# Gated mix of local attention and a mixture of experts on one core: inputs turned by DVE transposes in place of TensorE's, and the first expert prepared earlier

## The chip, the cores and the metric

The kernel runs on one core of one Trainium2 chip. The metric is the device time of one execution in microseconds (us), the median of the runs shown. PE is TensorE (PEld its weight loads), DVE is VectorE, ACT ScalarE, POOL GpSimd, SP SyncE; SP issues most DMAs and SPq is its DMA queue.

## The reference, cut to what matters

x has 2048 tokens of 512 features. `a` is a dilated local attention (32 heads of 16, a window of 8 at a step of 2), `b` a mixture of the best two of 8 experts with hidden size 1376; a gate mixes them.

```python
g = _sigmoid((x * gate_w).sum(-1, keepdims=True))
qkv = x @ wqkv                      # 512 x 1536, then attention per head
a = attention(qkv) @ wo             # 512 x 512
logits = xf @ w_gate                # 512 x 8
topk_idx = jnp.argsort(-logits, axis=-1)[:, :K]    # K = 2, gates by softmax
for e in range(E):
    h = _silu(xf @ w1[e]) @ w2[e]   # 512 x 1376, 1376 x 512
    out = out + w * h
return g * a + (1 - g) * b
```

## The kernel before, in words

Every float32 product is made of three: each operand is split into a high part (an ACT copy to the float32r type) and a low part (a DVE subtraction), and PE sums high by high, high by low and low by high. PE contracts over partitions, so x must be turned: features on partitions.

**Projection.** Four passes c = 0 to 3 over the 16 row blocks j of x (`qkv_mm` L230, 12 products a block, columns of 8 heads a pass; pass 0 also has the router's and the gate's 10 columns). In pass 0 each block is loaded (`load_x` L114, two blocks a DMA, two buffers), turned by four PE transposes into PSUM and split (`trans_x` L216, two blocks ahead of its products). `load_w` (L124) brings the weights of a pass in four DMAs into one buffer, `split_w` (L201) splits them during the pass before. SP's queue runs in program order (L131 to L135, L192 to L199, L810 to L825): first x and the weights, then the table and halo stores, which wait for POOL's memsets, then more x, the weights of pass 1, the stores of the staged results (L255) and the clearing of the accumulator (L199). POOL loads the gate weights (L141, L142) after one iota and before its other constants. Pass 0's first product needs them, split by `split_wg` (L209). ACT copies each block's result to a staging tile (`qkv_evac` L240); for c > 0 and j < 8 two of the three lie in the memory of the x buffers.

**Routing** runs on DVE in pass 1 (`route_a`, `slots`, `table`, `route_c`); `TQ` holds, for each slot of an expert, row numbers of quarter rows of x, `TG` whole rows.

**Attention** is a list of DVE steps (`att_steps` L513, eight rounds, mostly 2.29 us a step), dealt out between other work by `att_fill` (L579): it keeps a model clock for PE and for DVE, adds the PE time and the DVE time that the caller names, and emits steps until DVE's clock has reached PE's:

```python
clk["dve"] = max(clk["dve"], clk["pe"] - IDLE) + dve
clk["pe"] += pe
while not attn["done"] and clk["dve"] < clk["pe"]:
```

**Experts.** Eight experts in the order ORD = [3, 0, 1, 2, 4, 5, 6, 7], 11 units each (88 units, 0 to 87; a unit is 128 hidden columns). In unit i PE does the first product of unit i + 1 (`g1_mm`, 12 products for 512 tokens), then the second of unit i (`g2_mm`); ACT applies silu twice and DVE makes the low half of the hidden tile (`g1_act` L756). `prep_w1`, `prep_w2` copy weights on ACT and queue the subtractions in `LO`, which `los` (L696) emits. `gather_x` (L647) fetches an expert's tokens on POOL's queue and `prep_x` (L669) turns and splits them, during units 3 to 7 of the expert before. Both have two ways: for the first four experts of the order (`DVT` L46) four gathers of quarter rows and a 32x32 block transpose on DVE; for the last four one gather of whole rows and four PE transposes. The first expert is prepared in pass 3: its first weights are loaded at (c, j) = (3, 0) (L857 to L860), its blocks turned from j = 11 (L869), and unit 2's first weights after the pass (L909).

**End.** In unit 87 the steps of attention that are left are emitted (L941), ACT and DVE split the first two blocks of the attention output (`split_o` L900), then ACT scales the last expert's outputs (`y_out` L780) and POOL adds them into `acc_d`. `acc_d` is loaded back (L969), PE multiplies by wo (`wo_mm` L976, 16 blocks), DVE mixes and SP stores (`mix` L988).

Of the kernel before, what the change touches and what calls it, by code (L numbers as in the profile page):

```python
# [7 lines left out]
F32 = mybir.dt.float32  # L8
# [18 lines left out]
E = 8  # L27
# [11 lines left out]
CRPAD, PAPAD = 160, 64  # L39
# [5 lines left out]

DVT = ORD[:4]  # L46
T_T = 0.43
# [11 lines left out]
def kernel(  # L59
# [41 lines left out]

    phT = ExitStack()
# [10 lines left out]

    def load_x(j0, n):  # L114
        t = pa2.tile([P, 2, D], F32, tag="xr", bufs=2, name=f"xr{j0}")
        nc.sync.dma_start(t[:, :n], xt[:, j0:j0 + n])
        for i in range(n):
            XR[j0 + i] = (t, i)

    NW = [394, 384, 384, 384]  # L120
    wq = wqkv.rearrange("(k p) (t c) -> p k t c", p=P, t=3)
    WR, WH, WL = {}, {}, {}

    def load_w(c, ks=range(KD)):  # L124
        if 0 in ks:
            WR[c] = pa.tile([P, KD, 384], F32, tag="wr", bufs=1, name=f"wr{c}")
        for k in ks:
            nc.sync.dma_start(WR[c][:, k].rearrange("p (t c) -> p t c", t=3),
                              wq[:, k, :, c * P:(c + 1) * P])
# [7 lines left out]

    ii = at.tile([P, P], I32, name="ii", tag="acc")
    nc.gpsimd.iota(ii, pattern=[[1, P]], base=0, channel_multiplier=-1)
    wgr = cp.tile([P, KD, 10], F32, name="wgr")  # L140
    nc.gpsimd.dma_start(wgr[:, :, 0:8], w_gate.rearrange("(k p) e -> p k e", p=P))  # L141
    nc.gpsimd.dma_start(wgr[:, :, 8:9], gate_w.rearrange("(k p o) -> p k o", p=P, o=1))  # L142
    nc.gpsimd.memset(wgr[:, :, 9:10], 0.0)
# [12 lines left out]
    ident = cp.tile([P, P], F32, name="ident")  # L156
    nc.vector.tensor_scalar(ident, ii, 0.0, None, op0=OP.is_equal)
    before = cp.tile([P, P], BF, name="before")
    nc.vector.tensor_scalar(before, ii, 0.0, None, op0=OP.is_gt)
# [40 lines left out]

    def split_w(c, k):  # L201
# [14 lines left out]
    def trans_x(j):  # L216
        t, i = XR[j]
        p = ph(f"px{j}")
        for k in range(KD):
            nc.tensor.transpose(p[:, k * P:(k + 1) * P], t[:, i, k * P:(k + 1) * P], ident)  # L220
        pool = pa2 if j < 8 else pa
        XH[j] = pool.tile([P, KD * P], F32R, name=f"xh{j}")
        XL[j] = pool.tile([P, KD * P], F32R, name=f"xl{j}")
        nc.scalar.activation(XH[j], p, AF.Copy)
        nc.vector.tensor_tensor(XL[j], p, XH[j].bitcast(F32), op=OP.subtract)
# [200 lines left out]
    def table():  # L426
# [6 lines left out]
        V.tensor_scalar(TG, tk[:, 1], float(-NJ), float(S - 1), op0=OP.add, op1=OP.min)  # L433
# [172 lines left out]
    def load_w1(R, i):  # L606
# [4 lines left out]
        if R not in DVT:  # L611
            nc.sync.dma_start(t[:, :, :cols],
                              w1[bass.ds(e, 1), :, f0 * P:f0 * P + cols].rearrange("e (k p) f -> p (e k) f", p=P))
        for a in range(4 if R in DVT else 0):
            nc.sync.dma_start(t[32 * a:32 * a + 32, :, :cols],
                              w1[bass.ds(e, 1), a * P:(a + 1) * P, f0 * P:f0 * P + cols].rearrange("e (k q) f -> q (e k) f", q=32))
# [15 lines left out]
    TG = cp.tile([P, E * NB], I32, name="TG")  # L632
# [14 lines left out]
    def gather_x(R, b):  # L647
        t = cr.tile([P, 4, P], F32, tag="xg", bufs=4, name=f"xg{R}_{b}")
        col = NB * R + b
        XG[R, b] = t  # L650
        if R not in DVT:
            n = blocks(R)[b]
            nc.gpsimd.indirect_dma_start(
                out=t.rearrange("p t c -> p (t c)")[:n], out_offset=None, in_=xf,
                in_offset=bass.IndirectOffsetOnAxis(ap=TG[:n, col:col + 1], axis=0))
            return
        for T in range(-(-blocks(R)[b] // 32)):
            nc.gpsimd.indirect_dma_start(  # L658
                out=t[:, T], out_offset=None, in_=xq,
                in_offset=bass.IndirectOffsetOnAxis(ap=TQ[:, T, col:col + 1], axis=0))  # L660

# [7 lines left out]
    def prep_x(R, b):  # L669
# [4 lines left out]
        if R not in DVT:  # L674
            n = blocks(R)[b]
            t = XG[R, b].rearrange("p t c -> p (t c)")
            p = ph(f"pg{R}_{b}")
            for k in range(KD):
                nc.tensor.transpose(p[:, k * P:k * P + n], t[:n, k * P:(k + 1) * P], ident[:n, :n])  # L679
            pv = p.rearrange("p (k t) -> p k t", k=KD)[:, :, :n]  # L680
            s = slice(b * P, b * P + n)
            nc.scalar.activation(XGH[R][:, :, s], pv, AF.Copy)
            V.tensor_tensor(XGL[R][:, :, s], pv, XGH[R][:, :, s].bitcast(F32), op=OP.subtract)
            return
# [9 lines left out]
    LO = []  # L694
# [116 lines left out]
    for j in range(NJ):  # L811
# [97 lines left out]
    prep_w1(*units[2])  # L909
    los()  # L910
    next_w1(*units[2])
    g1_mm(*units[0])
    g1_act(*units[0], 0)
    for i, (R, f) in enumerate(units):
# [32 lines left out]
        first = T_MM * 12 if C <= 512 else 12 * (C / 2400 + 2 * T_HALF)  # L947
        att_fill(FILL * (first + second))
# [8 lines left out]
        if new_x:  # L957
            prep_x(NEXT[R], f - 3)
# [3 lines left out]
        att_fill((1 - FILL) * (first + second) + (T_T if new_x and NEXT[R] not in DVT else 0.0), T_S + 0.1 + (T_S * (1 + (NEXT[R] in DVT)) if new_x else 0.0))  # L962
# [123 lines left out]
```

## Time and profile before

| | us |
|---|---|
| median of 3 runs (729.88 to 734.13) | 731.86 |
| the profiled execution, its own time | 731.6 |
| its span | 729.8 |
| PE, DVE, ACT, POOL busy | 711.4, 598.7, 339.6, 204.8 |
| TensorE's granted clock, mean over the span (1 is full speed) | 0.992 |

The span is what the profile covers; 1.8 us of the execution's time lie around it. Busy times overlap. A row in order of time gives start, duration, engine, line, operation and tiles, and in brackets how long the engine had been idle and what released it. Matmuls are pipelined: successive ones start closer together than one lasts.

### The profile page before, as it was taken

To read this page: it belongs to the slowest core of one execution; us is meant where nothing else is said; L and a number is where in the kernel's file an instruction comes from. 1 tells how busy PE (TensorE), PEld (TensorE's weight loads), DVE (VectorE), ACT (ScalarE), POOL (GpSimd) and SP (SyncE) were. 2 spreads that over 40 slices of the span, in tenths; PEclk is the share of its full clock that TensorE was granted. 3 is DMA by queue.
4 is the path that set the end of the run, shared out by engine and by line. 5 is a ranking of instruction groups with operands and counts; after the bars stand their busy time and mean duration, and the time that the engine had idled before them with its cause. 6 is when DMAs were issued, how large, how long until landed. Compare 5 with 4: busy or idle time off the path is not lost.

```text
span 729.8 us, 10775 instructions
## 1 busy us (share of the span) xinstructions
PE 711.4 (97%) x3748; PEld 627.1 (86%) x3748; DVE 598.7 (82%) x728; ACT 339.6 (47%) x775; POOL 204.8 (28%) x217
## 2 busy tenths in 40 slices
PE   8999999959999999999999999999999999999996
PEld 7999999958889998999899988888888888888875
DVE  3247799778799988998899999979997999795474
ACT  4443233244645445534553554455446344734531
POOL 3000055062445460731082018206412300300400
PEclk9999999979999999999999999999999999999999
DMA  6668845939386637754675347664665633721592
GB/s 192 183 208 269 219 123 146 251 104 227 101 199 116 154 88 176 136 137 98 166 143 155 122 119 171 185 165 91 166 175 168 132 111 105 154 60 64 79 352 89
DMA packets 81448, 111.34 MB, mean 153 GB/s; under 512 B 7200, under 2 KB 54672, under 8 KB 81008
## 3 DMA queue, kind: packets, MB, share of 16 engines
q1 hardware_dynamic: 73008, 93.21, 45.2%
q0 software_dynamic: 8384, 17.43, 13.1%
q8 instruction: 30, 0.49, 0.3%
q14 instruction: 26, 0.21, 0.1%
HBM read 80.82 MB, written 29.78 MB: 152 GB/s over the span
## 4 chain that ended last, share of the span: by engine, by line
PE 82%; DVE 7%; DMA 6%; issue 2%; ACT 2%; SPq 0%; POOL 0%; DVEq 0%; ACTq 0%; POOLq 0%
PE phh L742 32%; PE py L772 10%; PE py L773 10%; PE py L775 10%; PE pq L237 4%; PE pq L236 4%; PE pq L238 4%; DVE lg L527 2%; DVE pr L524 1%; DMA w2r<-in_B_w_dram 1%; PE pa L984 1%; PE pa L985 1%; PE pa L986 1%; DMA w1r<-in_B_w_dram 1%; PE pg L679 1%
## 5 line engine op out<-in xcount | busy, mean ns | idle before, releaser
L794 POOL DMA_INDIRECT acc_d<-ysb,TI x35 | 94.2, 2691 | 251.5 <-ACT ysb L787 244.2
L772 PE MATMUL py<-w2h,hs 128*128 128x512 f32 (+1 forms) x352 | 138.9, 395 | 0.0
L773 PE MATMUL py<-w2l,hs 128*128 128x512 f32 (+1 forms) x352 | 137.5, 391 | 0.0
L753 ACT ACTIVATE hs<-phh 128x512 fp32r<-128x512 f32 (+7 forms) x121 | 55.8, 489 | 138.7 <-PE phh L742 136.4
L742 PE MATMUL phh<-xgh,w1h 128*128 128x512 f32 (+7 forms) x484 | 99.6, 338 | 8.3 <-ACT xgh L689 7.5
L658 POOL DMA_INDIRECT xg<-in_A_x_dram,TQ x69 | 81.3, 1179 | 89.7 <-DVE xraw L688 69.2
L742 PE MATMUL phh<-xgl,w1h 128*128 128x512 f32 (+7 forms) x484 | 99.3, 338 | 0.0
L742 PE MATMUL phh<-xgh,w1l 128*128 128x512 f32 (+7 forms) x484 | 99.2, 338 | 0.0
L742 PEld LDWEIGHTS phh<-xgh,w1h 128*128 128x128 f32 (+1 forms) x484 | 78.8, 187 | 20.9 <-ACT xgh L689 7.8
L775 PE MATMUL py<-w2h,hs 128*128 128x512 f32 (+1 forms) x352 | 94.2, 389 | 0.0
L756 DVE TENSOR_TENSOR hs<-hsf,hs 128x512 fp32r<-128x512 f32 (+1 forms) x88 | 60.3, 685 | 35.4 <-ACT hsf L755 35.1
L236 PE MATMUL pq<-wh,xh 128*128 128x384 f32 (+1 forms) x256 | 87.7, 343 | 0.0
L722 ACT ACTIVATE w2h<-w2r 128x512 fp32r<-128x512 f32 (+1 forms) x88 | 55.5, 631 | 68.4 <-PE py L775 43.7
L237 PE MATMUL pq<-wl,xh 128*128 128x384 f32 (+1 forms) x256 | 86.2, 337 | 0.2 <-DVE wl L207 0.2
L238 PE MATMUL pq<-wh,xl 128*128 128x384 f32 (+1 forms) x256 | 86.1, 336 | 0.0
L742 PEld LDWEIGHTS phh<-xgl,w1h 128*128 128x128 f32 (+1 forms) x484 | 77.5, 187 | 9.4
L742 PEld LDWEIGHTS phh<-xgh,w1l 128*128 128x128 f32 (+1 forms) x484 | 77.5, 187 | 9.4
L775 PEld LDWEIGHTS py<-w2h,hs 128*128 128x128 f32 (+1 forms) x352 | 66.1, 188 | 13.9
L772 PEld LDWEIGHTS py<-w2h,hs 128*128 128x128 f32 (+1 forms) x352 | 66.1, 188 | 12.7
L773 PEld LDWEIGHTS py<-w2l,hs 128*128 128x128 f32 (+1 forms) x352 | 66.2, 188 | 12.6
L524 DVE TENSOR_TENSOR pr<-qt,kt 128x2048 f32<-128x2048 f32 x32 | 72.7, 2288 | 5.0 <-DMA kt<-qkv 4.6
L527 DVE TENSOR_REDUCE lg<-pr 128x128 f32<-128x2048 f32 x32 | 72.7, 2278 | 0.0
(189 smaller groups left out, 1085.6 us busy)
## 6 DMA issues: line engine op xcount, KB each, us to landing
w2r<-in_B_w_dram SPq DMA_DIRECT2D x40, 512.0 KB, 5.2
qkv<-stg SPq DMA_DIRECT2D x24, 512.0 KB, 4.8
w1r<-in_B_w_dram SPq DMA_DIRECT2D x48, 192.0 KB, 4.5
w1r<-in_B_w_dram SPq DMA_DIRECT2D x12, 768.0 KB, 5.0
kt<-qkv SPq DMA_DIRECT2D x32, 156.0 KB, 6.1
vt<-qkv SPq DMA_DIRECT2D x32, 156.0 KB, 5.7
acc_d<-zer SPq DMA_DIRECT2D x16, 256.0 KB, 4.3
qt<-qkv SPq DMA_DIRECT2D x32, 128.0 KB, 6.0
```

The lines of the kernel that those rows point to most:

```text
L236: nc.tensor.matmul(p[:, :n], XH[j][:, s], WH[c][:, k, :n], start=(k == 0), stop=False)
L237: nc.tensor.matmul(p[:, :n], XH[j][:, s], WL[c][:, k, :n], start=False, stop=False)
L238: nc.tensor.matmul(p[:, :n], XL[j][:, s], WH[c][:, k, :n], start=False, stop=(k == KD - 1))
L524: V.tensor_tensor(pr, qb, custom(k, 4 * u * DH, [[2 * DH, 2], [1, 1024]]), op=OP.mult)
L527: V.tensor_reduce(lg[:, :, 2 * u - 2:2 * u].rearrange("p a w -> p w a"), prs[u - 1].rearrange("p w (a d) -> p w a d", d=16), axis=AX.X, op ...
L658: nc.gpsimd.indirect_dma_start(out=t[:, T], out_offset=None, in_=xq, in_offset=bass.IndirectOffsetOnAxis(ap=TQ[:, T, col:col + 1], axis=0))
L742: nc.tensor.matmul(t[:m, :n], w[:, k, :m], xx[:, k, o:o + n], start=(k == 0 and i == 0), stop=(k == KD - 1 and i == 2))
L756: V.tensor_tensor(hs[:m, 640:1152], s[:m, :512], hs[:m, :512].bitcast(F32), op=OP.subtract)
L772: nc.tensor.matmul(y[b], hs[:m, b * P:(b + 1) * P], wh[:m], start=st, stop=False)
L773: nc.tensor.matmul(y[b], hs[:m, b * P:(b + 1) * P], wl[:m], start=False, stop=False)
L775: nc.tensor.matmul(y[b], hs[:m, 640 + b * P:640 + (b + 1) * P], wh[:m], start=False, stop=sp)
L794: d = nc.gpsimd.indirect_dma_start(out=acc_d, out_offset=bass.IndirectOffsetOnAxis(ap=TI[:n, NB * R + b, 0:1], axis=0), in_=s[:n], in_offs ...
```

## The change

x, the projection's weights and the gate weights are loaded in four DMAs of 32 partitions where one had 128, so that each row block lies in SBUF as 32x32 squares; a DVE transpose in place of four PE transposes turns it (`trans_x`), and ACT and DVE split it from SBUF. Half of pass 0's weights are issued by ACT. The gate weights are issued by POOL ahead of its iota, in eight DMAs. `ident` and `before` are made at j = 4. All experts are gathered by quarters and turned by DVE; `DVT`, `TG` and `T_T` are gone. In an expert's unit `prep_x` now stands at the unit's start, its subtraction goes through `LO`, and DVE's clock is charged in `prep_x` and `los` (T_S = 0.69 each). The first expert's weights are loaded at (2, 6), (2, 8), (2, 10), (2, 12), its blocks prepared from (3, 8), its first weights split from (3, 10), with the loads that follow one block later.

```diff
-CRPAD, PAPAD = 160, 64
+CRPAD, PAPAD = 136, 64
...
-DVT = ORD[:4]
-T_T = 0.43
...
+    xj = xf.rearrange("(t i j) (a c) -> a j i t c", t=4, i=32, a=4)
...
     def load_x(j0, n):
-        t = pa2.tile([P, 2, D], F32, tag="xr", bufs=2, name=f"xr{j0}")
-        nc.sync.dma_start(t[:, :n], xt[:, j0:j0 + n])
+        t = pa2.tile([P, 2, 4, P], F32, tag="xr", bufs=2, name=f"xr{j0}")
         for i in range(n):
-            XR[j0 + i] = (t, i)
+            for a in range(4):
+                nc.sync.dma_start(t[32 * a:32 * a + 32, i], xj[a, j0 + i])
+            XR[j0 + i] = t[:, i]
...
         for k in ks:
-            nc.sync.dma_start(WR[c][:, k].rearrange("p (t c) -> p t c", t=3),
-                              wq[:, k, :, c * P:(c + 1) * P])
+            for a in range(4):
+                (nc.scalar if (c, ks[0]) == (0, 0) else nc.sync).dma_start(
+                    WR[c][32 * a:32 * a + 32, k].rearrange("p (t c) -> p t c", t=3), wq[a, k, :, :, c * P:(c + 1) * P])
...
+    wgr = cp.tile([P, KD, 10], F32, name="wgr")
+    for a in range(4):
+        nc.gpsimd.dma_start(wgr[32 * a:32 * a + 32, :, 0:8], w_gate.rearrange("(a k q) e -> a q k e", a=4, k=KD)[a])
+    for a in range(4):
+        nc.gpsimd.dma_start(wgr[32 * a:32 * a + 32, :, 8:9], gate_w.rearrange("(a k q o) -> a q k o", a=4, k=KD, o=1)[a])
+    nc.gpsimd.memset(wgr[:, :, 9:10], 0.0)
     ii = at.tile([P, P], I32, name="ii", tag="acc")
     nc.gpsimd.iota(ii, pattern=[[1, P]], base=0, channel_multiplier=-1)
-    wgr = cp.tile([P, KD, 10], F32, name="wgr")
-    nc.gpsimd.dma_start(wgr[:, :, 0:8], w_gate.rearrange("(k p) e -> p k e", p=P))
-    nc.gpsimd.dma_start(wgr[:, :, 8:9], gate_w.rearrange("(k p o) -> p k o", p=P, o=1))
-    nc.gpsimd.memset(wgr[:, :, 9:10], 0.0)
...
     def trans_x(j):
-        t, i = XR[j]
-        p = ph(f"px{j}")
-        for k in range(KD):
-            nc.tensor.transpose(p[:, k * P:(k + 1) * P], t[:, i, k * P:(k + 1) * P], ident)
...
-        nc.scalar.activation(XH[j], p, AF.Copy)
-        nc.vector.tensor_tensor(XL[j], p, XH[j].bitcast(F32), op=OP.subtract)
+        b = XR[j].rearrange("p t (k q) -> p t k q", k=KD)
+        nc.vector.transpose(b, b)
+        b = b.rearrange("p t k i -> p k t i")
+        h, l = (t.rearrange("p (k t i) -> p k t i", k=KD, t=4) for t in (XH[j], XL[j]))
+        nc.scalar.activation(h, b, AF.Copy)
+        nc.vector.tensor_tensor(l, b, h.bitcast(F32), op=OP.subtract)
...
     def prep_x(R, b):
...
-        if R not in DVT:
-            n = blocks(R)[b]
-            t = XG[R, b].rearrange("p t c -> p (t c)")
-            p = ph(f"pg{R}_{b}")
-            for k in range(KD):
-                nc.tensor.transpose(p[:, k * P:k * P + n], t[:n, k * P:(k + 1) * P], ident[:n, :n])
...
-            return
         n = -(-blocks(R)[b] // 32)
...
+        clk["dve"] += T_S
         nc.scalar.activation(XGH[R][:, :, s], raw, AF.Copy)
-        V.tensor_tensor(XGL[R][:, :, s], raw, XGH[R][:, :, s].bitcast(F32), op=OP.subtract)
+        LO.append((XGL[R][:, :, s], raw, XGH[R][:, :, s]))
...
-            if (c, j) == (3, 0):
-                for i in range(2):
-                    load_w1(ORD[0], i)
-                    load_w2(ORD[0], i)
+            if c == 2 and j in (6, 8, 10, 12):
+                (load_w1 if j % 4 == 2 else load_w2)(ORD[0], (j - 6) // 4)
             if (c, j) >= ATT0:
-                own = T_S if c < 3 and j in SPLIT[c] else 0.0
-                if c == 3 and j > 10:
-                    own += T_S * 2
-                att_fill(T_P, own)
+                att_fill(T_P, T_S if c < 3 and j in SPLIT[c] else 0.0)
...
-            if c == 3 and j > 10:
-                if j - 11 < len(blocks(ORD[0])):
-                    prep_x(ORD[0], j - 11)
-                if j >= 12:
-                    u = units[(j - 12) // 2]
-                    prep_w1(*u) if j % 2 == 0 else prep_w2(*u)
-                    los()
-                    next_w1(*u) if j % 2 == 0 else next_w2(*u)
+            if c == 3:
+                los()
+                for g, u in NEXTW.pop(j - 1, ()):
+                    g(*u)
+                if 8 <= j < 8 + len(blocks(ORD[0])):
+                    prep_x(ORD[0], j - 8)
+                if 10 <= j < 15:
+                    u = units[(j - 10) // 2]
+                    a, b = (prep_w1, next_w1) if j % 2 == 0 else (prep_w2, next_w2)
+                    a(*u)
+                    NEXTW[j] = ((b, u),)
+    los()
     phA.close()
...
-    prep_w1(*units[2])
-    los()
-    next_w1(*units[2])
     g1_mm(*units[0])
...
+        if new_x:
+            prep_x(NEXT[R], f - 3)
         att_fill(FILL * (first + second))
         los()
...
-        if new_x:
-            prep_x(NEXT[R], f - 3)
         g2_mm(R, f, i)
...
-        att_fill((1 - FILL) * (first + second) + (T_T if new_x and NEXT[R] not in DVT else 0.0), T_S + 0.1 + (T_S * (1 + (NEXT[R] in DVT)) if new_x else 0.0))
+        att_fill((1 - FILL) * (first + second), T_S + 0.1)
```

## Rows read from the trace of the kernel before

**Rows 1.** The page, part 1: busy us, share of the span, instructions.

```profile
PE 711.4 (97%) x3748; PEld 627.1 (86%) x3748; DVE 598.7 (82%) x728; ACT 339.6 (47%) x775; POOL 204.8 (28%) x217
```

**Rows 2.** Windows: busy PE, PEld, DVE, ACT, POOL, then granted clock, DMA share, GB/s.

```profile
154.00:156.00 2.00, 0.00 (x0) 0.00 (x0) 1.67 (x3) 1.31 (x5) 1.54 (x2) 0.62 0.16 47
```

**Rows 3.** PE in order of time at the first expert's start.

```profile
159.57 2.08 PE L742 MATMUL phh<-xgh,w1h 128*128 128x512 f32 x4 [7.49 <-ACT xgh L689]
...
164.79 0.40 PE L742 MATMUL phh<-xgh,w1h 128*128 128x512 f32 x1
```

**Rows 4.** DVE in order of time before it.

```profile
138.40 1.23 DVE L559 TENSOR_TENSOR o<-acc 128x1024 f32<-128x1024 f32 x1
144.26 2.29 DVE L524 TENSOR_TENSOR pr<-qt,kt 128x2048 f32<-128x2048 f32 x1 [4.64 <-DMA kt<-qkv]
```

**Rows 5.** The chain that ended last, at unit starts: start, us, what.

```profile
446.77 2.72 PE phh L742 x12
...
452.21 2.72 PE phh L742 x12
...
458.12 2.72 PE phh L742 x12
```

**Rows 6.** PE in order of time in pass c = 0, and pass 1's first product.

```profile
7.28 0.43 PE L236 MATMUL pq<-wh,xh 128*128 128x394 f32 x1
...
41.42 0.60 PE L220 MATMUL px<-ident,xr 128*128 128x128 f32 x4
...
44.03 0.60 PE L220 MATMUL px<-ident,xr 128*128 128x128 f32 x4
...
48.81 0.33 PE L236 MATMUL pq<-wh,xh 128*128 128x384 f32 x1
```

**Rows 7.** Groups by line: busy us, mean ns; the last line: KB, us to landing.

```profile
L688 DVE STREAM_TRANSPOSE xraw<-xg 128x512 f32<-128x512 f32 x16 | 11.2, 702 | 0.0
L690 DVE TENSOR_TENSOR xgl<-xraw,xgh 128x512 fp32r<-128x512 f32 x16 | 11.1, 692 | 11.2 <-ACT xgh L689 11.2
L689 ACT ACTIVATE xgh<-xraw 128x512 fp32r<-128x512 f32 x16 | 10.1, 632 | 45.0 <-DVE xraw L688 45.0
L141 POOL DMA_DIRECT2D wgr<-in_B_w_gate_dram x1 | 1.0, 977 | 0.4 <-issue 0.4
L854 POOL DMA_DIRECT2D ovx<-ovx_i x1 | 0.6, 571 | 89.1 <-DVE rt_ad L478 89.1
wgr<-in_B_w_gate_dram POOLq DMA_DIRECT2D x1, 16.0 KB, 3.7
```

**Rows 8.** SP's issues: ns min/median/max by line; landing of expert weight quarters; stores in time.

```profile
L116 SPq DMA_DIRECT2D xr<-in_A_x_dram x9: 328/362/1152, 0.8 to 34.4; - x9
L510 SPq DMA_DIRECT2D kt<-qkv x32: 302/419/1058, 73.5 to 561.8; - x32
L128 SPq DMA_DIRECT2D wr<-in_A_wqkv_dram x16: 545/665/1450, 1.2 to 89.0; - x16
w1r<-in_B_w_dram SPq DMA_DIRECT2D x16, 112.0 KB, 2.8
7.33 1.56 SPq L196 DMA_DIRECT2D qkv<-zer  x4
29.82 3.42 SPq L255 DMA_DIRECT2D qkv<-stg  x3
```

**Rows 9.** DVE in order of time at the end.

```profile
657.17 2.31 DVE L565 STREAM_TRANSPOSE ot<-o 128x2048 f32<-128x2048 f32 x1
...
674.30 0.69 DVE L756 TENSOR_TENSOR hs<-hsf,hs 96x512 fp32r<-96x512 f32 x1 [3.59 <-ACT hsf L755]
```

**Rows 10.** ACT in order of time at the end.

```profile
675.20 2.17 ACT L905 ACTIVATE oh<-ot 128x512 fp32r<-128x512 f32 x2
677.98 2.42 ACT L787 ACTIVATE ysb<-py,TI 128x512 f32<-128x512 f32 x4 [0.61 <-PE py L775]
```

**Rows 11.** PE in order of time in the product by wo.

```profile
698.91 0.47 PE L984 MATMUL pa<-woh,oh 128*128 128x512 f32 x1 [1.22 <-DVE ag L992]
```

More of the change, by code (lines that the diff above doesn't have):

```diff
@@ L100, in ph @@
         return ps.tile([P, 512], F32, tag="h", bufs=3, name=name)
+    NEXTW = {}
     phT = ExitStack()
@@ L112 @@
     XR = {}
+    xj = xf.rearrange("(t i j) (a c) -> a j i t c", t=4, i=32, a=4)
     def load_x(j0, n):
-        t = pa2.tile([P, 2, D], F32, tag="xr", bufs=2, name=f"xr{j0}")
-        nc.sync.dma_start(t[:, :n], xt[:, j0:j0 + n])
+        t = pa2.tile([P, 2, 4, P], F32, tag="xr", bufs=2, name=f"xr{j0}")
         for i in range(n):
-            XR[j0 + i] = (t, i)
+            for a in range(4):
+                nc.sync.dma_start(t[32 * a:32 * a + 32, i], xj[a, j0 + i])
+            XR[j0 + i] = t[:, i]
     NW = [394, 384, 384, 384]
-    wq = wqkv.rearrange("(k p) (t c) -> p k t c", p=P, t=3)
+    wq = wqkv.rearrange("(a k q) (t c) -> a k q t c", a=4, k=KD, t=3)
     WR, WH, WL = {}, {}, {}
@@ L155 @@
     keep_warm(NWARM)
[L156 to L159, printed above, removed]
     i8 = cp.tile([P, 16], F32, name="i8")
@@ L199, in clear_acc, with late_constants @@
         nc.sync.dma_start(acc_d[:S].rearrange("(p j) d -> p j d", p=P)[:, j], zer)
+    def late_constants():
+        nc.vector.tensor_scalar(ident, ii, 0.0, None, op0=OP.is_equal)
+        nc.vector.tensor_scalar(before, ii, 0.0, None, op0=OP.is_gt)
+    ident = cp.tile([P, P], F32, name="ident")
+    before = cp.tile([P, P], BF, name="before")
     def split_w(c, k):
@@ L223, in trans_x, with qkv_mm @@
         XL[j] = pool.tile([P, KD * P], F32R, name=f"xl{j}")
-        nc.scalar.activation(XH[j], p, AF.Copy)
-        nc.vector.tensor_tensor(XL[j], p, XH[j].bitcast(F32), op=OP.subtract)
+        b = XR[j].rearrange("p t (k q) -> p t k q", k=KD)
[4 more added lines that the diff above has]
+        nc.vector.tensor_tensor(l, b, h.bitcast(F32), op=OP.subtract)
     LG = cp.tile([P, NJ, 10], F32, name="LG")
     PQ, STG = {}, {}
-    def qkv_mm(c, j):
+    def qkv_mm(c, j, ks=range(KD)):
         n = NW[c]
-        p = py(f"pq{c}_{j}")
-        PQ[c, j] = p
-        for k in range(KD):
+        if ks[0] == 0:
+            PQ[c, j] = py(f"pq{c}_{j}")
+        p = PQ[c, j]
+        for k in ks:
             s = slice(k * P, (k + 1) * P)
@@ L432, in table @@
         V.tensor_tensor(tk[:, 1], tk[:, 1], p[:, :, 1], op=OP.add)
-        V.tensor_scalar(TG, tk[:, 1], float(-NJ), float(S - 1), op0=OP.add, op1=OP.min)
         V.tensor_scalar(TI[:, :, 0], tk[:, 1], float(-NJ), None, op0=OP.add)
@@ L610, in load_w1 @@
         t = cr.tile([P, KD, 384], F32, tag="w1r", bufs=2, name=f"w1r{R}_{i}")
-        if R not in DVT:
-            nc.sync.dma_start(t[:, :, :cols],
-                              w1[bass.ds(e, 1), :, f0 * P:f0 * P + cols].rearrange("e (k p) f -> p (e k) f", p=P))
-        for a in range(4 if R in DVT else 0):
+        for a in range(4):
             nc.sync.dma_start(t[32 * a:32 * a + 32, :, :cols],
@@ L631 @@
     TI = cp.tile([P, E * NB, 2], I32, name="TI")
-    TG = cp.tile([P, E * NB], I32, name="TG")
     TQ = cp.tile([P, 4, E * NB], I32, name="TQ")
@@ L649, in gather_x @@
         col = NB * R + b
-        XG[R, b] = t
-        if R not in DVT:
-            n = blocks(R)[b]
-            nc.gpsimd.indirect_dma_start(
-                out=t.rearrange("p t c -> p (t c)")[:n], out_offset=None, in_=xf,
-                in_offset=bass.IndirectOffsetOnAxis(ap=TG[:n, col:col + 1], axis=0))
-            return
         for T in range(-(-blocks(R)[b] // 32)):
@@ L660, in gather_x @@
                 in_offset=bass.IndirectOffsetOnAxis(ap=TQ[:, T, col:col + 1], axis=0))
+        XG[R, b] = t
     B = {}
@@ L673, in prep_x @@
             XGL[R] = pool.tile([P, KD, 576], F32R, tag="xgl", name=f"xgl{R}")
-        if R not in DVT:
-            n = blocks(R)[b]
-            t = XG[R, b].rearrange("p t c -> p (t c)")
-            p = ph(f"pg{R}_{b}")
-            for k in range(KD):
-                nc.tensor.transpose(p[:, k * P:k * P + n], t[:n, k * P:(k + 1) * P], ident[:n, :n])
[L680 to L684, printed above, removed]
         n = -(-blocks(R)[b] // 32)
@@ L688, in prep_x @@
         V.transpose(raw.rearrange("p k (t i) -> p t k i", i=32), XG[R, b][:, :n].rearrange("p t (k q) -> p t k q", k=KD))
+        clk["dve"] += T_S
         nc.scalar.activation(XGH[R][:, :, s], raw, AF.Copy)
-        V.tensor_tensor(XGL[R][:, :, s], raw, XGH[R][:, :, s].bitcast(F32), op=OP.subtract)
+        LO.append((XGL[R][:, :, s], raw, XGH[R][:, :, s]))
+    LO = []
     WS = {}
-    LO = []
     def los():
@@ L823 @@
             clear_acc(j - 8)
+        if j == 4:
+            late_constants()
         if j == 15:
```

## The prediction

> **What bounds the kernel now.** I read the busy shares first: PE is busy 97% of the 729.8 us span [rows 1], so a change pays where it shortens PE's own list, or where PE stands still. Next the windows and PE's instructions in order of time around 152 us, the only long standstill: the first product of the experts starts at 159.57, after 7.49 us idle (since 152.08) put down to the copy of the first expert's inputs. The granted clock averages 0.62 over 154 to 156, so it dropped from 2.4 to 1.2 GHz about 2.4 us after PE went idle; the first 12 products take 5.22 us (159.57 to 164.79) where such a group takes 2.72 elsewhere [rows 2, 3, 5]. That preparation was late because DVE, which does the 32x32 transposes between attention steps, stood 4.64 us for a key tile [rows 4], whose load is queued on SP behind four expert weight loads (L857 to L860). Last I read the two places where TensorE transposes, to see what four of them cost in the stream, and the end of the kernel.
>
> **The change, part by part.**
>
> *The last four experts, no transposes on PE.* A unit without them repeats every 5.44 us (446.77 to 452.21), one with them 5.91 (452.21 to 458.12) [rows 5]. There are 16 such blocks: 16 x 0.47 = **7.5 us gained**. What replaces them is 16 DVE transposes of 0.70 us [rows 7] and 48 more gathers on POOL, which is 28% busy [rows 1]; I cost the gathers at nothing, as the blocks of the first four experts are already fetched so: they are covered by the three units between gather and use, and without that cover the copies on ACT, and the tiles behind them, would wait for each. The DVE time comes back at the end (below).
>
> *First expert prepared from row block 8, its weights loaded in the third projection pass.* At best the 7.49 us gap and the slow clock, 5.22 - 2.72 = 2.5, go: 10.0 us. With the weight loads ahead of it on SP, the key tile is in time, and DVE goes on at 139.6 (138.40 + 1.23 [rows 4]). I walk its new list from there: four transposes at 0.70, two attention steps at 2.29, five subtractions at 0.69, two waits of 0.7 for ACT's copy [rows 4, 7]: 12.3, so the last input is ready at 151.9. PE wants it about 0.9 after 152, behind its first four products. The margin is 1 us; the low half of the first hidden tile then queues behind another attention step, about 1.2 us late. **Gain 8.8 us**; bounds 10.0 and 5. The lower is where the copy of block 0 waits for the store of the staging tile whose memory it takes over: the third preparation pass starts now one block after that store is issued and was four after.
>
> *Stage c = 0, loads by quarters.* Before, a block takes 2.61 us (41.42 to 44.03), with four transposes inside; its 12 products alone take 12 x 0.181 = 2.17, so PE gains 0.44 a block; the stage ends at 48.81 [rows 6]. Against that:
> - Start. The gate weights now come in 8 POOL DMAs. One of a single row holds POOL 0.57 us, the present one of 512 short rows 0.98 [rows 7]; a quarter has 128, nearest the first: 0.65. The eighth starts at 0.95 + 7 x 0.65 = 5.5; landing 3.7 later, as the present one does [rows 7], gives 9.2, and the first product 9.6 instead of 7.28. The warm-up products end at about 5, so PE idles longer than it had when the clock fell in [rows 2], and I take 5.2 us at half clock as in [rows 3]: block 0's 12 products take 4.3, block 1's 2.6, block 2 starts at 16.6; with no other wait block 8 would at 29.6.
> - SP's queue. A block is 4 issues instead of half an issue, a weight pass 16 instead of 4. No quarter of x is in the trace. The whole x load takes 0.36 us to issue, a key quarter 0.42, the projection's weight rows, with the same 512-byte pieces but three times as many, 0.665 [rows 8]. I take 0.42 with its gap, since a quarter has as many pieces as the whole x load has; the ends are 0.37 and 0.65. SP: 0.77; blocks 0, 1 to 4.1; half a weight pass 7.5; blocks 2, 3 10.9; table and halo stores 12.9; blocks 4 to 7 19.6; the 16 weight quarters of pass 1 26.3; the fourth quarter of block 8 issues at 27.6, lands 2.8 later [rows 8], and is transposed (0.74) and copied (0.66) by 31.9: PE waits 2.3. Blocks 10, 11 by 33.1; 12, 13 wait until block 9's tile is read (35.5), 38.8; then three staging stores, 3.4 [rows 8], and a clear: 43.2; block 14 is ready at 43.2 + 1.3 + 2.8 + 1.4 = 48.7. The stage ends at 48.7 + 2 x 2.17 = 53.0 to 53.4: **4.4 us lost**, not the 6.2 gained that 14 x 0.44 promises. About 84 issues stand ahead of block 14, so each 0.05 us of issue is 4.2 us: bounds 1 (0.37) and 14 or more (0.55 and over). What hides the stage's 16 DVE transposes is PE's 2.17 a block: the chain transpose, ACT's copy, subtraction takes 0.70 + 0.63 + 0.69 = 2.0 [rows 7], so the cover is thin.
>
> The page "DMA: Bandwidth & Descriptors" of the Trainium skill (Issuing engines are not separate DMA queues) says that the time to initiate a DMA is usually small relative to the DMA itself; by it the queue would not count, and the term would be rival C's. The same page (Rules for kernel authors) advises one 128-partition transfer over partial ones, which speaks against this change. That an issue holds SP for 0.36 us or more the rows show.
>
> *The end.* Attention is dealt out by the planner's clock (L577 to L594). For the 16 blocks it now charges DVE 0.69 more each and gives PE 0.43 less each: 17.9 us of its clock, 3.3 units of 5.46. Before, the last attention step, the transpose at 657.17 [rows 9], is dealt in unit 83 of 0 to 87. Stepping the clock through the new code, three attention steps remain around the last unit's low half: a full step (2.29), o (1.23) and the transpose (2.31), the last two by the forced drain at L941. In the old times: the low half ends at 674.99, or about 675.9 behind a full step; then 2.29, two subtractions for wo (1.38), 1.23 and 2.31 make 683.1. ACT copies the first two oh tiles only then, 2.17, and the last expert's outputs queue behind them: 685.2 instead of 677.98 [rows 9, 10]. From there scatter, reload and mix run as before, and PE, which waited for that mix at 698.91 [rows 11], is idle over 5 us, with the clock down, and meets the mix again about as late. **7.2 to 7.8, say 7.5 us lost**; bounds 6 (low half on time) and 8.7.
>
> Sum: -7.5 - 8.8 + 4.4 + 7.5 = -4.4. The profiled execution took 731.6 us, 0.26 below the median of the three runs: 727.2 on its own basis, **727.5** against the median.
>
> **Rivals.**
> - A, the gap comes back: preparation meets the staging store, or the DVE margin of 1 us is eaten, and half of the 8.8 goes. 731 to 732. For it: a thin margin, and ACT's projection copies queue behind the input copies. Against: PE has five output tiles, ten us of cover.
> - B, the other side: SP's issue sets stage c = 0. At 0.47 us a quarter the sum is nothing; at 0.55 the loss is 4.4 + 11 = 15 and the kernel takes about 738. For it: the 0.665 of rows with 512-byte pieces. Against: 384 pieces there, 128 here.
> - C, the queue hides: x is always there in time. Block 2 at 16.6 and 14 x 2.17 end the stage at 47.0, 1.8 earlier than before: 721.3. The skill's sentence above is this case; the table of issues above speaks against it.
> - D, the end is covered: DVE runs ahead of the planner's clock, and attention is done before the last products. Then 720. For it: before, the last step was dealt four units early, more than was needed. Against: DVE can't get ahead, as each low half waits for PE's products (3.59 us idle) [rows 9].
> - That the change doesn't do what it says could only be where DVE or SP, not PE, paces: B.
>
> **How the numbers follow.** A measurement of this kernel can tell about 0.5%, 3.7 us. The forecast case (724.5 to 730.5) has 0.45, 0.29 of it faster by over 0.5%; A 0.22, all within 0.5%; B 0.15, 0.14 of it slower by over 0.5%; C 0.10 and D 0.08, both faster. Faster 0.29 + 0.18 = 0.47, slower 0.14, same 0.16 + 0.22 + 0.01 = 0.39. The range 721 to 736 leaves out half of D and C and the worse half of B.
>
> **What would show it.** c = 1's first product at about 53 (48.81 before), with PE waiting for xh or wr around blocks 8 and 14; SP without idle time from 1 to 45; the first product near 9.6; no gap at the first expert; units at 5.44 throughout the last four experts; DVE's last transpose after the last unit's low half and PE idle some 5 us before L984. Wrong if stage c = 0 ends before 49 (C), after 58 (B), if a gap over 3 us remains at the first expert (A), or if PE passes into L984 without a wait (D).

## The result, and the profile after

The changed kernel takes 739.84 us (median of 6 executions), the kernel before 731.54 us in the same comparison: a ratio of 1.011, 95% interval 1.009 to 1.0132. It is 1.1% slower, where the forecast was 727.5 us, faster or the same. The profiled executions have spans of 738.0 and 729.8 us, 8.2 us apart, and these 8.2 us can be laid out by stage, read from the starts of PE's instructions in the two traces:

| us | before | after | change |
|---|---|---|---|
| first product of c = 1 starts | 48.81 | 68.55 | +19.7 |
| from there to the last product of the projection | 102.93 | 102.92 | 0.0 |
| from there to the experts' first product | 7.83 | 0.17 | -7.7 |
| from there to the experts' last product | 518.7 | 507.5 | -11.2 |
| from there to the last product by wo | 45.3 | 52.8 | +7.5 |
| from there to the end of the span | 6.3 | 6.1 | -0.2 |

Three of the four terms of the forecast came within 1.4 us of what was written; stage c = 0 lost 19.7 us instead of 4.4. The page, part 1, of the kernel after, to be held beside [rows 1]:

```profile
PE 707.2 (96%) x3620; PEld 621.0 (84%) x3620; DVE 617.2 (84%) x759; ACT 343.4 (47%) x775; POOL 273.5 (37%) x271
```

PE has 128 instructions fewer and is busy 4.2 us less in a span 8.2 us longer: it stands still 12.4 us more. PE in order of time in stage c = 0 after, its first product, the first of block 2, the two long gaps (blocks 8 and 11) and the first product of c = 1, against [rows 6]:

```profile
8.88 0.69 PE L246 MATMUL pq<-wh,xh 128*128 128x394 f32 x1 [3.77 <-ACT wh L219]
...
20.16 0.34 PE L246 MATMUL pq<-wh,xh 128*128 128x394 f32 x1
...
41.60 0.70 PE L246 MATMUL pq<-wh,xh 128*128 128x394 f32 x1 [8.25 <-ACT xh L233]
...
54.84 0.69 PE L246 MATMUL pq<-wh,xh 128*128 128x394 f32 x1 [3.92 <-ACT xh L233]
...
68.55 0.33 PE L246 MATMUL pq<-wh,xh 128*128 128x384 f32 x1
```

ACT is named, but it was not late by its own work. DVE in order of time before block 8: it waited 10 us for the x quarters, and behind them the chain of transpose, copy and subtraction takes 2.0 us a block, as reckoned:

```profile
40.18 0.71 DVE L230 STREAM_TRANSPOSE xr<-xr 128x512 f32<-128x512 f32 x1 [10.02 <-DMA xr<-in_A_x_dram]
41.59 0.69 DVE L234 TENSOR_TENSOR xl<-xr,xh 128x512 fp32r<-128x512 f32 x1 [0.70 <-ACT xh L233]
42.24 0.71 DVE L230 STREAM_TRANSPOSE xr<-xr 128x512 f32<-128x512 f32 x1
```

The transfers were issued late. SP's queue in order of time (start, duration of the whole row of issues), and the durations of one issue by line (ns, minimum, median, maximum), against [rows 8]:

```profile
0.76 6.01 SPq L118 DMA_DIRECT2D xr<-in_A_x_dram  x8
6.82 5.17 SPq L131 DMA_DIRECT2D wr<-in_A_wqkv_dram  x8
12.11 3.83 SPq L118 DMA_DIRECT2D xr<-in_A_x_dram  x8
...
18.17 8.06 SPq L118 DMA_DIRECT2D xr<-in_A_x_dram  x16
26.28 10.29 SPq L131 DMA_DIRECT2D wr<-in_A_wqkv_dram  x16
36.66 12.02 SPq L118 DMA_DIRECT2D xr<-in_A_x_dram  x24
48.78 2.38 SPq L265 DMA_DIRECT2D qkv<-stg  x3
```

```profile
L118 SPq DMA_DIRECT2D xr<-in_A_x_dram x64: 311/430/1022, 0.8 to 58.8; - x64
L131 SPq DMA_DIRECT2D wr<-in_A_wqkv_dram x56: 584/595/1710, 6.8 to 117.9; - x56
```

SP issues with few pauses up to 52 us. Quarters of x follow each other every 0.48 to 0.50 us (3.83 over 8, 8.06 over 16), quarters of w every 0.64 (10.29 over 16). The first eight quarters of x came only every 0.75, and that is not issue time: one issue takes 0.31 to 0.55 us there, and each of the last five begins within 0.02 us of the landing of one of the weight quarters that ACT's queue issued, on whose semaphore it waits. SP's waits in this stage (us in total, times, longest):

```profile
SPq L118 <- DMA wr<-in_A_wqkv_dram: 2.4, 4, 1.2
```

The fourth quarter of block 8 is issued at 38.20, not at 27.6 as I had it:

```profile
38.20 0.42 SPq L118 DMA_DIRECT2D xr<-in_A_x_dram  x1
```

The three stores of the staged results stand behind 24 quarters until 48.78, and ACT, which must have their memory back for block 8's result, waits with the input copies of block 11 behind it. ACT in order of time:

```profile
52.23 0.28 ACT L258 ACTIVATE stg<-pq 128x128 f32<-128x128 f32 x1 [5.69 <-DMA qkv<-stg]
```

After each gap PE runs at a lower clock. Windows after (PE, PEld, DVE, ACT, POOL busy, then granted clock, DMA share, GB/s): the end of the gap before block 8 and what follows it, what follows the gap before block 11, and the rest of the stage:

```profile
36.00:41.60 5.60, 0.00 (x0) 0.00 (x0) 0.73 (x2) 0.68 (x2) 0.00 (x0) 0.59 0.42 120
41.60:46.80 5.20, 5.20 (x16) 4.97 (x17) 3.45 (x5) 2.87 (x13) 0.00 (x0) 0.50 0.45 129
54.84:60.60 5.76, 5.76 (x17) 5.53 (x18) 4.08 (x7) 3.33 (x15) 0.00 (x0) 0.50 0.58 182
61.00:68.50 7.50, 7.50 (x43) 7.50 (x42) 3.13 (x6) 4.03 (x16) 0.00 (x0) 1.00 0.46 173
```

A granted clock of 0.50 is the lower of the two levels, 1.2 GHz; the products there last 0.70 and 0.53 us where 0.34 is usual. Block 8 takes 4.2 us and block 9 2.8, block 11 4.2 and block 12 3.0, where a block at 2.4 GHz takes 2.17. The products of blocks 0 and 1 are as slow, up to 19.7, though the profile gives a granted clock of 1.00 there; why is left open. The 19.7 us by which c = 1 comes later are: 1.6 for the first product; 5.4 for blocks 0 and 1 (11.3 us to block 2's start, 5.8 before); 12.2 for the two gaps; 5.5 for the four slow blocks; less 5.0 for 14 blocks without transposes (35.7 us before, 14 x 2.19 after).

The gains are there. PE at the first expert, against [rows 3], has no gap and no slow clock:

```profile
171.64 1.09 PE L731 MATMUL phh<-xgh,w1h 128*128 128x512 f32 x4
```

The chain shows units in the last four experts at 5.44 us, where some took 5.91 in [rows 5]:

```profile
513.31 2.72 PE phh L731 x12
518.75 2.72 PE phh L731 x12
```

And the end, against [rows 9] to [rows 11]: DVE's last attention steps come after the last unit's low half, ACT's copies wait for them, and PE for these:

```profile
676.62 0.68 DVE L745 TENSOR_TENSOR hs<-hsf,hs 96x512 fp32r<-96x512 f32 x1
677.22 2.28 DVE L563 TENSOR_TENSOR acc<-acc,pv 128x2048 f32<-128x2048 f32 x1
679.42 1.28 DVE L886 TENSOR_TENSOR wol<-wor,woh 128x512 fp32r<-128x512 f32 x2
680.62 1.22 DVE L568 TENSOR_TENSOR o<-acc 128x1024 f32<-128x1024 f32 x1
681.88 2.31 DVE L574 STREAM_TRANSPOSE ot<-o 128x2048 f32<-128x2048 f32 x1
```

```profile
684.22 2.07 ACT L895 ACTIVATE oh<-ot 128x512 fp32r<-128x512 f32 x2 [8.01 <-DVE ot L574]
686.20 2.41 ACT L776 ACTIVATE ysb<-py,TI 128x512 f32<-128x512 f32 x4
```

```profile
685.36 0.79 PE L971 MATMUL pa<-woh,oh 128*128 128x512 f32 x1 [5.81 <-ACT oh L895]
```

### The profile page after: what moved, and what is told of

Its sections match the earlier page's. It is cut to its first block, busy times and chain, and to the rows that moved or that the text cites. A ratio compares the mean times of both kernels' runs of the same rounds, so it can differ in the third digit from the quotient of the medians.

```text
span 738.0 us, 11042 instructions
## 1 busy us (share of the span) xinstructions
PE 707.2 (96%) x3620; PEld 621.0 (84%) x3620; DVE 617.2 (84%) x759; ACT 343.4 (47%) x775; POOL 273.5 (37%) x271
## 3 DMA queue, kind: packets, MB, share of 16 engines
q0 software_dynamic: 9344, 17.43, 12.4%
## 4 chain that ended last, share of the span: by engine, by line
PE 87%; SPq 4%; DVE 4%; DMA 2%; issue 2%; ACT 1%; ACTq 0%; DVEq 0%
PE phh L731 33%; PE py L762 10%; PE py L761 10%; PE py L764 10%; PE pq L246 5%; PE pq L247 5%; PE pq L248 5%; SPq L118 2%; PE pa L971 2%; PE pa L973 2%; PE pa L972 2%; SPq L131 2%; PE py L767 1%; PE py L766 1%; DVE pv L559 1%
## 5 line engine op out<-in xcount | busy, mean ns | idle before, releaser
L656 POOL DMA_INDIRECT xg<-in_A_x_dram,TQ x133 | 168.7, 1268 | 76.9 <-DVE xraw L676 36.4
L246 PE MATMUL pq<-wh,xh 128*128 128x384 f32 (+1 forms) x256 | 91.2, 356 | 17.3 <-ACT xh L233 12.4
L247 PE MATMUL pq<-wl,xh 128*128 128x384 f32 (+1 forms) x256 | 90.3, 353 | 0.0
L248 PE MATMUL pq<-wh,xl 128*128 128x384 f32 (+1 forms) x256 | 89.6, 350 | 0.0
L761 PEld LDWEIGHTS py<-w2h,hs 128*128 128x128 f32 (+1 forms) x352 | 66.1, 188 | 13.1
```

The source lines that it names most:

```text
L656: nc.gpsimd.indirect_dma_start(out=t[:, T], out_offset=None, in_=xq, in_offset=bass.IndirectOffsetOnAxis(ap=TQ[:, T, col:col + 1], axis=0))
L761: nc.tensor.matmul(y[b], hs[:m, b * P:(b + 1) * P], wh[:m], start=st, stop=False)
```

## The experiments

The theory was that the number of DMAs issued by SP sets stage c = 0 (rival B of the prediction). Its rivals: DVE's chain, the 512-byte pieces, or another part of the change. The runs fell on three chips. On one the kernel before took 737.37 us: stage c = 0 as before, the second pass's weights issued by POOL, the number of issues alone, and the early preparation the first time. On the second it took 731.32: the attention dealt earlier (two runs), the stores on POOL too, and the kernel before unchanged. On the third it took 731.97: the other four. Ratios are to the before of the same chip. Three of the runs on SP's queue (POOL's weights, the number of issues, the stores on POOL) and the kernel before unchanged are one execution each and are read by their stages; the other times are medians of four or six.

**Stage c = 0 as before, all else as changed.** Whole loads and TensorE transposes come back:

```diff
...
-        nc.vector.transpose(b, b)
...
+        for k in range(KD):
+            nc.tensor.transpose(p[:, k * P:(k + 1) * P], t[:, i, k * P:(k + 1) * P], ident)
...
```

> The changed kernel with the whole first stage (c=0) as it was before: whole loads of x and w, transposes on TensorE, the gate weights in two loads; the expert and preparation parts stay changed. If the loss sits in stage c=0 alone, as the two traces say (c=1's first product 48.81 -> 68.55 us), it goes back to 48.8 +- 1 us, the gap before the first expert stays near 0.2 us, the end keeps its 52.7 us, and the time is 739.8 - 19.7 = about 720 us (718 to 722). Rival: the early preparation or the new experts cost what stage c=0 seems to cost, or the late stages take back what the early one gives: c=1 starts at 49 but the time stays above 728 us.

Measured: 721.48 us, ratio 0.9776 (0.9756 to 0.9795); c = 1's first product at 49.16, no gap at the first expert, 53.85 us for the end. The loss lies in stage c = 0: every later stage agrees with that of the changed kernel within 1.1 us.

**The second pass's weights issued by POOL.**

```diff
-                (nc.scalar if (c, ks[0]) == (0, 0) else nc.sync).dma_start(
+                (nc.scalar if (c, ks[0]) == (0, 0) else nc.gpsimd if c == 1 else nc.sync).dma_start(
```

> The changed kernel with the 16 quarters of the second pass's weights issued by POOL's queue in place of SP's, nothing else. Theory (SP's issue time sets the stage): SP held 10.29 us of w issues between the quarters of block 7 and of block 8; without them the x quarters go on at 26.3 us, the 8.24 us gap before block 8 and the 3.9 us gap before block 11 go, with the half clock after them, c=1's first product moves from 68.55 to 50 to 56 us, and the time is 722 to 728 us. Rival (the chain transpose, ACT copy, DVE subtract, or the landing of 512-byte pieces sets the pace of a block): c=1's first product stays at 64 us or later and the time at 735 us or more.

Measured: 730.94 us, c = 1's first product at 59.55, 9.0 us earlier for 10.3 us of issues moved. The same DMAs, with the same pieces, are issued by another queue, and the stage is shorter by nearly what their issues took. Block 8's gap is gone; the other is not, and both c = 1 and the time lie between the two expectations. ACT in order of time shows why, the stores being still behind 40 quarters on SP:

```profile
43.24 0.28 ACT L258 ACTIVATE stg<-pq 128x128 f32<-128x128 f32 x1 [5.81 <-DMA qkv<-stg]
```

**The number of issues alone, in the kernel before.** Four loads of 32 partitions for one, with pieces of 2 KB and the transposes on TensorE:

```diff
-        nc.sync.dma_start(t[:, :n], xt[:, j0:j0 + n])
         for i in range(n):
+            for a in range(4):
+                nc.sync.dma_start(t[32 * a:32 * a + 32, i], xt[32 * a:32 * a + 32, j0 + i])
...
```

> The kernel before with each load of x (by blocks) and of w in stage c=0 and after split into four loads of 32 partitions, on the queues of the changed kernel; layout, pieces of 2 KB and the transposes on TensorE stay. It has the number of issues of the changed kernel without its DVE chain and without its 512-byte pieces. Theory by the number of issues (0.475 us a quarter of x, 0.64 us a quarter of w): c=1's first product goes from 48.81 to 60 us or later and the time from 731.5 to 742 us or more. Rival one (DVE chain or pieces): c=1's first product stays below 51 us, the time within 2 us of before. Rival two (an issue costs by the pieces it describes, so that a quarter of 32 pieces takes a quarter of the whole load's 0.33 us): SP's x quarters take under 0.2 us each and c=1 starts below 52 us.

Measured: 757.18 us, c = 1's first product at 67.49, 18.7 us later than before. SP's queue in order of time, and one issue by line, read as those of the kernel after:

```profile
18.04 8.50 SPq L118 DMA_DIRECT2D xr<-in_A_x_dram  x16
26.64 10.16 SPq L131 DMA_DIRECT2D wr<-in_A_wqkv_dram  x16
36.90 12.51 SPq L118 DMA_DIRECT2D xr<-in_A_x_dram  x24
```

```profile
L118 SPq DMA_DIRECT2D xr<-in_A_x_dram x64: 310/419/1642, 0.8 to 59.0; - x64
```

This decides it: neither DVE's chain nor short pieces are in this kernel, and its stage c = 0 loses as much, 18.7 us. The two stages end 1.1 us apart (68.55 and 67.49); that doesn't say what DVE's chain costs, since both wait for SP. The rest of the longer time lies in other waits, among them units of 10.2, 7.5 and 7.4 us where some 6.3 are usual. A quarter of 32 pieces holds SP as long as one of 128: 419 and 430 ns.

**The early preparation alone, in the kernel before.** The loads at (2, 6) to (2, 12), the preparation from (3, 8), the first expert's subtractions through `LO`; run twice, the second time because of the chip's own before:

> The kernel before with one part of the change, the first expert's loads at blocks 6 to 12 of pass 2 and its preparation from block 8 of pass 3 on. Theory (the 7.49 us gap and the half clock after it go, and nothing takes their place): the gap at the first expert falls to 0.2 us, the first unit from 10.67 to 8.2 us, the time from 731.5 to about 721.5 us (720 to 723). Rival (the planner deals the attention later, or ACT and DVE give it back): first expert starts early but the time stays above 726 us.

> The kernel before with the early preparation alone, once more, for the same reason. Theory (by its trace the span is 8.2 us shorter: gap and half clock 10.1 us, less 1.9 us of new waits in two units): about 723 us, a ratio of 0.987 to 0.991. Rival (the ratio 0.9825 measured first holds): 718.5 us.

Measured: 724.54 us, ratio 0.9825 (0.9808 to 0.9843), and 726.48 us, ratio 0.992 (0.9901 to 0.994), each a little slower than expected. In both the gap at the first expert is 0.2 us, a gain of 7.7 and some 2.4 in the first unit; two later units give part back, 8.11 and 8.41 us long in the first run, 7.86 and 9.95 in the second, where 6.38 and 6.32 are usual, and in the second run c = 1 came 1.6 us later (50.42). ACT in order of time before the longer one: the copy for attention's exponential changes ACT's table twice, just ahead of silu, and PE waits 1.85 us.

```profile
336.57 1.28 ACT L537 ACT_TABLE_LOAD   x1
337.99 0.63 ACT L537 ACTIVATE lg<-lg 128x512 f32<-128x512 f32 x1
338.64 1.28 ACT L758 ACT_TABLE_LOAD   x1
339.94 0.70 ACT L758 ACTIVATE hs<-phh 128x280 fp32r<-128x280 f32 x2
```

So the part is a gain, 0.8% in the second pair, a little less than the trace of the first promised. The 1.75% of the first pair go with the 737.37 us of the kernel before on that chip.

**The kernel before, unchanged**, to see what made the 737.37 us:

> The kernel before, unchanged, with a profile on this chip, where it took 737.4 us in place of 731.5 us. Theory one (a stall that comes or goes with the chip, like the units of 10.17 and 7.46 us that the run with quarters alone showed): the stages agree with the trace of before within 0.5 us but for a few units or one gap that make 5 to 6 us. Theory two (something spread evenly, a clock or the memory): every stage is 0.8% longer.

Measured: 731.7 us. It ran on another chip, where before takes 731.32, and its stages agree with the first trace within 0.5 us, so it doesn't answer the question.

**The first run's kernel again**, for the same reason:

> The first run's kernel once more, because the chip it ran on gave 737.4 us for the kernel before in place of 731.5 us. Theory (its stages by the trace: c=1's first product at 49.16, the units 10.9 us shorter than those of the preparation alone, the end at 53.85 us): about 720 us (718 to 722) on a chip where before takes 731.5 us, a ratio of 0.982 to 0.987. Rival (the ratio 0.978 measured there holds): 715 us.

Measured: 722.46 us, ratio 0.9872 (0.9848 to 0.9896), just above the band of the theory; not the rival's 715. Against the preparation alone on the same chip, the DVE experts, with `prep_x` at the unit's start, are worth 4.0 us there (726.48 less 722.46) and 3.1 on the first (724.54 less 721.48).

**The DVE experts alone, in the kernel before.**

```diff
-DVT = ORD[:4]
+DVT = ORD
```

> The kernel before with the last four experts' rows also loaded by quarters and turned by DVE, nothing else. Theory (the transposes on TensorE go, 16 of 0.47 us, and come back at the end, where the attention's last steps are dealt into the last unit): units 7.5 to 8.7 us shorter, PE's gap of some 6 us before the output products, the time 730 to 732 us. Rival (the late end comes from the early preparation or from stage c=0): no gap at the end, 723 to 724 us.

Measured: 736.71 us, ratio 1.0059 (1.004 to 1.0079). A miss in size on both sides, with `prep_x` still where it was in the unit: from the experts' first to their last product 6.2 us less, the end 11.1 longer (56.4 from the experts' last product to the last by wo), and c = 1 2.1 later in that execution. PE in order of time:

```profile
682.50 0.80 PE L984 MATMUL pa<-woh,oh 128*128 128x512 f32 x1 [8.26 <-ACT oh L905]
```

The late end comes with the DVE experts and not with the early preparation, which by itself ends in 44.9 and 45.9 us.

**The attention dealt earlier.** The first run's kernel with the planner's cost of a step times 0.98, then 0.96:

```diff
-SLACK = 1.0
+SLACK = 0.98
```

> The first run (stage c=0 as before, the rest as changed) with the planner counting each attention step at 0.98 of its cost, so that it deals the last step some 8 us earlier. Theory of the end (attention's last steps were dealt into the last unit, and ACT's copies for the output product wait for them): PE's 5.8 us gap before the output products falls below 1 us, the end from 53.85 to 46 to 47 us, and the time by 6 to 8 us to 714 us (713 to 716). Rival (DVE's own total of work, not the dealing, sets the end): the gap stays above 3 us, or DVE comes late in the units and they grow by as much; the time stays at 719 us or more.

> The same with 0.96, so that the last step is dealt some 16 us earlier. Theory: no more to gain at the end (46 us), and DVE, which takes 2.24 us for a step counted at 2.20, falls behind by at most some 6 us over the phase, and a few units wait for its subtractions: within 2 us of the run with 0.98, rather above it. Rival (the dealing isn't the cause): as the first run, 721 us.

Measured: 712.79 us, ratio 0.9744 (0.9727 to 0.9761), and 715.07 us, ratio 0.9774 (0.9757 to 0.9791). With 0.98 the last transpose on DVE stands before the last low half, and PE goes from the experts into the product by wo with no wait:

```profile
654.06 2.30 DVE L563 STREAM_TRANSPOSE ot<-o 128x2048 f32<-128x2048 f32 x1
656.29 0.69 DVE L734 TENSOR_TENSOR hs<-hsf,hs 96x512 fp32r<-96x512 f32 x1
```

```profile
659.55 1.07 PE L753 MATMUL py<-w2h,hs 96*128 96x512 f32 x4
660.46 0.40 PE L958 MATMUL pa<-woh,oh 128*128 128x512 f32 x1
```

The end takes 45.5 us where the first run's kernel took 53.85, and the time is just below the expected 713. With 0.96 the end takes 44.9, two units wait, for 0.58 and 1.26 us, and the time is 2.3 us above that with 0.98, a little more than expected. **0.98 is the best version of the study**, 2.6% faster than the kernel before on its chip.

**The stores on POOL too**, with the second run's edit:

```diff
-                nc.sync.dma_start(dst, STG[t].rearrange("p h j d -> p h (j d)"))
+                (nc.gpsimd if c == 0 and j == 7 else nc.sync).dma_start(dst, STG[t].rearrange("p h j d -> p h (j d)"))
```

> The run before it (second pass's weights issued by POOL) with the three stores after block 7 on POOL's queue too. Theory (SP's queue again: there the three stores stood behind 40 x quarters until 39.8 us, and ACT's copy of block 8 waited 5.81 us for them, which made the 5.47 us gap before block 11): the gap goes with the half clock after it, c=1's first product moves from 59.55 to 51 to 53.5 us and the time from 730.9 to 722 to 725 us. Rival (the landing of the x quarters or the DVE chain makes that gap): it moves by less than 2 us, the time by less than 2 us.

Measured: 727.59 us, c = 1's first product at 55.01, 4.5 us earlier: less than expected, and the time misses its 722 to 725. The gap fell from 5.46 to 2.02 us and not to nothing: issued at 35.22, the stores still reach ACT late.

```profile
35.22 2.69 POOL L265 DMA_DIRECT2D qkv<-stg  x3 [11.62 <-ACT stg L258]
```

```profile
39.52 0.28 ACT L258 ACTIVATE stg<-pq 128x128 f32<-128x128 f32 x1 [2.35 <-DMA qkv<-stg]
```

**Two queues for x.** From block 4 on two quarters of four, and the second pass's weights one k at a time, on POOL, with 0.98:

```diff
...
-                nc.sync.dma_start(t[32 * a:32 * a + 32, i], xj[a, j0 + i])
+                (nc.gpsimd if j0 >= 4 and a >= 2 else nc.sync).dma_start(t[32 * a:32 * a + 32, i], xj[a, j0 + i])
...
-        if j == 1:
-            load_w(1)
+        if j in (1, 3, 5, 7):
+            load_w(1, (j // 2,))
```

> The changed kernel with two of the four x quarters from block 4 on, and the second pass's weights one k at a time from blocks 1, 3, 5 and 7, on POOL's queue, the stores back on SP's, and the planner's 0.98. Theory (once no queue is late, what is left of stage c=0 is the late first blocks, 20.2 us at block 3 against 15.7, and the shorter blocks, 2.15 us against 2.6): no gap after block 3, c=1's first product at 48 to 50.5 us, as early as with whole loads and transposes on TensorE, the time 712 to 715 us. Rival (DVE's chain or the pieces of 512 bytes bound the stage): blocks of 2.6 us or gaps, c=1's first product at 54 us or later and 718 us or more.

Measured: 718.77 us, ratio 0.9818 (0.98 to 0.9836); c = 1's first product at 55.03. A miss: the rival's numbers came, though its cause only in part. The expectation also took block 2's start (20.2 us after, 13.1 before) for block 3's. The x quarters are no bound any more after block 3: DVE waits for them 0.2 us at most between blocks 4 and 9. What is left is the start (block 3 at 22.8 us, 15.7 before), 2.34 us of gap behind the stores, issued from 35.88, and DVE's chain where weights are split within it. DVE in order of time:

```profile
45.62 0.56 DVE L215 TENSOR_TENSOR wl<-wr,wh 128x384 fp32r<-128x384 f32 x1 [0.28 <-ACT wh L214]
46.10 0.70 DVE L230 STREAM_TRANSPOSE xr<-xr 128x512 f32<-128x512 f32 x1
47.50 0.69 DVE L234 TENSOR_TENSOR xl<-xr,xh 128x512 fp32r<-128x512 f32 x1 [0.70 <-ACT xh L233]
48.11 0.70 DVE L230 STREAM_TRANSPOSE xr<-xr 128x512 f32<-128x512 f32 x1
49.52 0.69 DVE L234 TENSOR_TENSOR xl<-xr,xh 128x512 fp32r<-128x512 f32 x1 [0.70 <-ACT xh L233]
50.49 0.56 DVE L215 TENSOR_TENSOR wl<-wr,wh 128x384 fp32r<-128x384 f32 x1 [0.29 <-ACT wh L214]
```

Two blocks take 4.87 us there (45.62 to 50.49), or 2.43 each, hardly less than the 2.61 with transposes on TensorE. So this version still ends stage c = 0 5.4 us after the one with whole loads and 0.98 (49.63). At block 3 it is already 6.5 us late (22.8 against 16.3), and the stores' gap adds 2.3; the blocks between give some back. What is lost lies in the start, with its quarter loads, and in the stores, and not in turning x on DVE, whose blocks are no slower than those with transposes on TensorE. No run mends the start.

## Why the prediction was wrong

**The step that failed is SP's queue in stage c = 0.** The mechanism was in the walk, issue by issue, but a quarter was costed at 0.42 us "with its gap", for x and for weights. Measured: 0.48 to 0.50 from one x quarter to the next, 0.64 for a weight quarter. At block 8 the walk was already 10.6 us early; 5.4 of these are the 24 weight quarters, about half. The nearest row was taken for the wrong reason: the number of pieces was thought to set the cost of an issue, so the 0.665 of the present weight load, with 384 pieces, was set aside; but a weight quarter with 96 pieces takes 0.595, almost as much, and the quarters of 32 and 128 pieces take the same. A weight quarter should have been priced from the weight row, and the range taken up to it.

**Four things were not in the walk.** SP's first x quarters waited 2.4 us in all for the landing of weight quarters that ACT issued. The late second half of pass 0's weights, issued by 12.0 and not by 7.5, held up ACT's copies of them by 1.2 and 2.1 us during block 0, and the products of blocks 0 and 1 ran slow for 10.8 us where 5.2 were reckoned: block 2 started at 20.16 and not at 16.6. The stores were put in SP's order, but ACT's wait for them, with the input copies queued behind it, was not: 3.92 us of gap at block 11. And the slow clock after a gap was charged for neither gap: 5.5 us. Rival B had the sign and the place, and it had 15 in 100. Its 738 us at 0.55 us an issue is near the 739.84 measured in part by luck: it counts nothing but issues, and two of these four, the stores and the clock, come to 9.4 us.

The Trainium skill's sentence on the time to initiate a DMA ("DMA: Bandwidth & Descriptors", Issuing engines are not separate DMA queues) was rival C. One issue is indeed shorter than its DMA here, 0.43 us of SP for 64 KB that land in 2.0 us. But the DMAs overlap and SP's issues follow one another, so that the queue did count: the run with the number of issues alone shows it at c = 1's first product, 18.7 us later. The same page's advice on one 128-partition transfer (Rules for kernel authors) is borne out, though its reason there is that the parts share the DMA engines, and what the runs here show is the time to issue them.

**The other terms, point by point.**
- Last four experts, 7.5 us: right. The 11.2 us between the experts' first and last product are 2.5 of the first unit, some 1.1 of a stall in a unit at 352 us that went too, and about 7.5 for the 16 blocks.
- First expert, 8.8 us: 7.7 and 2.5, just over the upper bound. Rival A is out: no gap is left.
- The end, 7.5 us lost: 7.5, by the steps written; with 0.98 the end takes 45.5 us, 45.3 before, which shows that the dealing caused it, and rival D is out.
- The first product: 8.88, for 9.6. The last of the gate weights landed at 8.5, a little before the 9.2 reckoned, and ACT copied them then.
- Of the signs named ahead, no gap at the first expert, units at 5.44, the late last transpose, PE's wait before the products by wo and a busy SP were all seen; c = 1 after 58 was named as rival B's.

## What to carry to other kernels

Where a change multiplies the number of DMAs, walk each queue issue by issue and price each kind from the row of its own kind: four quarters of a weight load took 2.4 us of issue where the whole took 0.67, eight of x 3.4 where a load of two blocks took 0.36, and all that stood behind them on the queue, stores too, came late. After each gap that this makes, charge the slow clock too. What a part is worth depends on what stands beside it: the DVE experts alone cost 0.6% here, were worth 3 to 4 us on top of the earlier preparation, and the two together gained another 8.3 us at the end (53.85 to 45.5) once an attention step was counted at 0.98 of its cost. When a change bundles three ideas, time each one alone.

## What was not expected of the hardware

- An issue costs by the DMA and hardly by the number of its pieces: 419 ns for 32 pieces of 2 KB, 430 for 128 of 512 bytes, 362 for a whole two-block load [rows 8]. Weight loads cost more, whole or quartered (665 and 595 ns); what of them does it wasn't tried. POOL took 565 ns for the same quarter and 545 for a weight quarter (run with two queues, run with POOL's weights).
- The first eight quarters on SP took 6.01 us, 3.83 the next eight. ACT's queue issued eight weight quarters in the same stretch, 0.76 to 6.0, and SP stood 2.4 us for their landings, 2.6 and 2.7 in the runs with POOL's weights and with the number of issues alone: two queues that issue at once aren't independent where their DMAs use the same semaphores in turn.
- On one of the chips the kernel before took 737.37 us, on the others 731.5; the variants run on both kinds (721.48 and 722.46, 724.54 and 726.48) were not slower there. Why is left open.
